# DMA transposes for normalised rows in a two-layer transformer kernel on one Trainium2 core

## The chip, the core and the metric

The kernel runs on one core of a Trainium2 chip. The core has a matrix engine (TensorE, PE in the profile; its weight loads are PEld), a vector engine (VectorE, DVE), an activation engine (ScalarE, ACT), GpSimd (POOL) and a queue engine (SyncE, SP) that issues DMAs here. The engines run side by side, each works off its own instructions in order, and they wait for one another through semaphores. SBUF is the on-chip memory, PSUM the smaller memory into which the matrix engine writes. The metric is the device time of one execution in microseconds (us).

## What is computed

Two layers on x of 2048 rows by 448 columns in bf16; both layers use the same weights. Each layer adds self-attention with 16 heads of 28, and then a two-matrix MLP with a squared relu:

```python
def _layernorm(x, axis=-1, eps=1e-5):
    m = jnp.mean(x, axis=axis, keepdims=True)
    v = jnp.var(x, axis=axis, keepdims=True)
    return (x - m) / jnp.sqrt(v + eps)

# A: softmax(q k^T * Dh**-0.5) v, all heads, times wo
# B: h = x @ w1 + b1;  h = max(h, 0)**2;  h @ w2 + b2
x = x + A(_layernorm(x));  x = x + B(_layernorm(x))
x = x + A(_layernorm(x));  x = x + B(_layernorm(x))
```

## The kernel before

**Tiles.** The 2048 rows are 16 row tiles of 128. Four row tiles make a block of 512 rows; layer 1 cuts its last block in two of two row tiles each. x stays in SBUF (`x_sb`). Heads are padded to 32 rows and lie four to a group, so there are four groups (`g`).

**Attention.** Scores are made transposed: for each group of heads, each block of queries and each key tile, PE multiplies K with Q (L531) into `sc`, a PSUM tile that takes three products of 512 columns. There are two such tiles. ACT takes the exponential of one whole tile, 128x1536, into `pt` (L546); this happens 683 times. PE then multiplies `pt` with V (L581) and sums over keys in one PSUM bank, `oT`. The softmax's denominator comes out of the same product, from a column of ones in V. When a pass ends, DVE takes `oT` out (L605, L607), and norm_stream divides: the denominators go out and come back by three small DMAs on SP's queue (`dn`, L638; `scr`, L650; `rec`, L657) with a reciprocal on DVE between (L644), or, for the last block of a layer, over PE and a wide reciprocal on DVE (L623, L629). L667 multiplies.

**The rest of a block.** chain(l, qb) starts when four groups are divided: the output projection with `wo` for each row tile and the addition to x on DVE (L678), layernorm(), the first MLP matrix with relu (L707 on DVE, L705 on ACT) and square (L714), the second matrix and its addition, and then, in layer 0, another layernorm() and the projections to K, V and Q of layer 1. All these matmuls go through mm_tile() and have the line L405. They share one PSUM bank, `mt` (resource R_m); the score tiles serve them too only before the first and after the last exponential.

**layernorm().** For each row tile DVE takes the moments (L309, L310). One reciprocal square root by Newton steps on DVE serves all row tiles of the block (L319 to L328). L372 writes the normalised row into one of four buffers `xn`. For each pair of row tiles, turn() lets PE transpose eight 128x128 pieces into the PSUM bank as `tp` (L347), and DVE or ACT copies them to `xnT` (L357, L355), which is what the next matmuls read. The four `xn` buffers are held in pairs (resource R_xn).

**What sets the order.** The program's order on each engine is written by a planner inside the kernel. Streams (scores, exponentials, PV, loads, chains and so on) yield operations with an engine, a price in us, dependencies, and resources that they acquire and release. The planner keeps a clock per engine and always emits the operation that could start first, by priority where two could; work on PE has to end near the time at which the next scores are due. So a price changes where an operation stands, not how long it takes. DMAs have the extra latency `LAT["DMA"]` of 2.0 and their own `lat`. All DMAs are issued on SP's queue, one after another, each after its own wait.

**Heat.** The stream heat() adds matmuls without use (L750, they read `xn0` and the identity) where the planned load of PE over the last 2.8 us is under 0.74.

**Loads.** loads() issues x of the first block, wqkv, x of the other blocks, and then wo, w1, b1, w2, b2, all at the start.

Of the kernel before, what the change touches and what calls it, by code (L numbers as in the profile page):

```python
# [10 lines left out]
DT = mybir.dt  # L11
AF = mybir.ActivationFunctionType
ALU = mybir.AluOpType
P = 128
# [9 lines left out]
AHEAD = range(2)  # L24
SLACK = 0.6
WINDOW = 2.8


class Res:
# [9 lines left out]


class Op:
    __slots__ = ("eng", "dur", "fn", "deps", "acq", "rel", "mode", "sets", "start", "end", "res", "turn", "ready", "lat")

    def __init__(self, eng, dur, fn, deps=(), acq=None, rel=None, mode="full", sets=(), lat=0.0):
# [8 lines left out]
LAT = {"PE": 0.22, "ACT": 0.22, "DVE": 0.10, "POOL": 0.15, "DMA": 2.0}  # L53


class Planner:
# [1 line left out]


    def __init__(self):  # L60
        self.clock = {"PE": 0.0, "ACT": 0.0, "DVE": 0.0, "POOL": 0.0, "DMA": 0.0}
        self.mode = None
        self.tok = {}
        self.streams = []
        self.past = []
# [35 lines left out]
    def run(self):  # L101
        while self.streams:
            cands = []
            for st in self.streams:
                s, e = self.earliest(st[2]) if st[2] is not None else (None, None)
                if s is not None:
                    cands.append((s, st[0], e, st))
            assert cands, "no stream can go on"

            due = next((c[3][2].ready for c in cands if c[1] == 0), None)  # L110
            if due is None:
                due = next((c[0] + c[3][2].dur + LAT["ACT"] for c in cands if c[1] == 1), None)
# [12 lines left out]
            if e == "PE":  # L125
                self.mode = o.mode
                self.past = [p for p in self.past if p[1] > s - 8.0] + [(s, o.end)]
            o.fn(e) if o.fn else None
            for a in o.rel:
                a.res.rel[a.turn] = o.end + LAT[e]  # L130
            for key in o.sets:
                self.tok[key] = o
            st[2] = next(st[1], None)
            if st[2] is None:
                self.streams.remove(st)
# [3 lines left out]
def kernel(  # L139
# [12 lines left out]
    nc = tc.nc  # L152
# [95 lines left out]
    def loads():  # L248
        kb = 1024
        yield dma(x_sb[:, 0:2, :], x_view[:, 0:2, :], 224 * kb, ("x", 0, 0))  # L250
        yield dma(x_sb[:, 2:4, :], x_view[:, 2:4, :], 224 * kb, ("x", 0, 1))
        qk_main = A_wqkv[0:3 * P, 0:2 * D].rearrange("(c p) n -> p c n", p=P)
        yield dma(st_qk[:, 0:3, :], qk_main, 680 * kb, ("wqk", 0))
        yield dma(st_qk[0:DL, 3, :], A_wqkv[3 * P:D, 0:2 * D], 112 * kb, ("wqk",))
        v_main = A_wqkv[0:3 * P, 2 * D:3 * D].rearrange("(c p) n -> p c n", p=P)
        yield dma(wv[:, 0:3, :], v_main, 340 * kb, ("wv", 0))
        yield dma(wv[0:DL, 3, :], A_wqkv[3 * P:D, 2 * D:3 * D], 56 * kb, ("wv",))
        for b in range(1, NTB // 4):
            for hf in range(2):
                t0 = 4 * b + 2 * hf  # L260
                yield dma(x_sb[:, t0:t0 + 2, :], x_view[:, t0:t0 + 2, :], 224 * kb, ("x", b, hf))
        for hh in range(G):
            yield dma(wo[DHP * hh:DHP * hh + DH, :, :],
                      A_wo.rearrange("(g hh r) d -> hh r g d", hh=G, r=DH)[hh], 98 * kb, ("wo", hh))
        yield dma(w1[:, 0:3, :], B_w1[0:3 * P, :].rearrange("(c p) n -> p c n", p=P), 1344 * kb, ("w1", 0))
        yield dma(w1[0:DL, 3, :], B_w1[3 * P:D, :], 224 * kb, ("w1", 1))
        yield dma(w1[DL:DL + 1, 3, :], B_b1.rearrange("(o f) -> o f", o=1), 30 * kb, ("w1",))
        yield dma(w2[:, :, :], B_w2.rearrange("(c p) d -> p c d", p=P), 1568 * kb, ("w2",))
        yield dma(b2w[0:1, :], B_b2.rearrange("(o d) -> o d", o=1), 30 * kb, ("b2",))
# [28 lines left out]

    s_left = [True]

    def layernorm(t0, nt, deps_of, early=False):


        mv = sp.tile([P, 4, 2], DT.float32, name="mv")
        last = None
        for j in range(nt):
            def stats(e, j=j):
                st = sp.tile([P, 6], DT.float32, name="st")
                nc.vector.bn_stats(out=st[:, :], in_=x_sb[:, t0 + j, :])  # L309
                nc.vector.bn_aggr(out=mv[:, j, :], in_=st[:, :])  # L310
            last = Op("DVE", 0.80, stats, deps=deps_of(j))
            yield last
        rstd = sp.tile([P, 4], DT.float32, name="rstd")

        def rsqrt(e):
# [46 lines left out]

        for p0 in range(0, nt, 2):
            js = range(p0, min(p0 + 2, nt))
            own = Op("DVE", 0.0, None, acq=R_xn)
            yield own
            xs = []
            for j in js:
                xn = xns[2 * (own.turn % 2) + j % 2]

                def norm(e, j=j, xn=xn):
                    nc.vector.tensor_scalar(out=xn[:, 0:D], in0=x_sb[:, t0 + j, :],  # L372
                                            scalar1=mv[:, j, 0:1], scalar2=rstd[:, j:j + 1],
                                            op0=ALU.subtract, op1=ALU.mult)
                nm = Op("DVE", 0.42, norm, deps=[rs])
                yield nm
                xs.append((xn, nm))

            todo.append((p0, own, xs))
            if early and p0 + 2 < nt:  # L380
                continue
            while todo:
                p0, own, xs = todo.pop(0)
                yield from turn(p0, own, xs)
# [92 lines left out]

    def first_block(blk):
        early = blk == 0
        xnT, own_xt, ends = yield from layernorm(4 * blk, 4, lambda j: [("x", blk, j // 2)] + ([] if early else [GATE[blk]]), early)  # L480
        yield from qkv(0, 4 * blk, 4, xnT, own_xt, ends, early)


# [56 lines left out]
    def e_stream():  # L540
        for gi, us in enumerate(groups):
            n = len(us) * 512

            def fn(e, gi=gi, n=n):
                pt = gbuf[gi]["pt"] = ptp.tile([P, 3 * 512], DT.bfloat16, name="pt")
                nc.scalar.activation(out=pt[:, 0:n], in_=gbuf[gi]["sc"][:, 0:n], func=AF.Exp, scale=scale)  # L546
            o = gbuf[gi]["e"] = Op("ACT", n / 1200 + 0.092, fn, deps=[("s", gi)], acq=R_pt,
                                   rel=gbuf[gi]["s"], sets=("e", gi))
            yield o

# [3 lines left out]
    def p_stream():  # L554
# [11 lines left out]
        for si, ((pi, kb), parts) in enumerate(steps):  # L566
# [8 lines left out]
            def fn(e, kb=kb, parts=parts, box=box, opens=opens, l=l, g=g, kbs=kbs, r=r, n=n):  # L575
                if opens:
                    box["t"] = ps_o.tile([P, QB], DT.float32, name="oT")
                for i in range(r):
# [5 lines left out]
                                         start=(kb + i == kbs[0]), stop=(kb + i == kbs[-1]),  # L584
                                         tile_position=(0, DHP * hh))
            gis = sorted({p[0] for p in parts})
            o = Op("PE", 0.24 + 0.01 * r, fn,
                   deps=[("e", gis[-1]), *{("V", l, kb + i) for i in range(r)}],
                   acq=R_o if opens else None,
                   rel=[gbuf[gi]["e"] for gi in gis if last_use[gi] == si], mode="col")  # L590
# [90 lines left out]
    def chain(l, qb):  # L681
# [13 lines left out]
        yield own_h  # L695
        hacts = []
# [23 lines left out]
        ys = []  # L720
# [75 lines left out]
```

## Time and profile before

| what | value |
|---|---|
| runs | 973.53, 973.73, 972.98 us; median 973.53 |
| the profiled execution | 972.86 us, of which its span on the core 971.1 us |
| granted TensorE clock, mean | 0.993 |
| transposes on PE, L347 | 256 of 128x128, 20.2 us busy |
| scores, L531 | 269.3 us busy on PE |
| PV, L581 | 206.2 us busy on PE |
| matmuls without use, L750 | 291, 93.2 us busy |
| relu on DVE, L707 | 99, 691 ns each |
| moments, L309 and L310 | 64 each, 602 and 182 ns |
| DMA | 16.75 MB, mean 17 GB/s; 273 GB/s in the first fortieth of the span |

The page gives for each group of instructions the busy time and the mean of one, then the idle time of its engine just before it and what ended most of that. Instructions overlap at their ends, so a mean can be longer than the distance from one start to the next. A timeline line gives the start, the time until the last of the merged instructions ended, engine and line, the tiles, the count, and in brackets the idle time before it with its releaser. SPq lines are the issues on SP's queue. In the view by stretch, each pair is busy time and count for PE, PEld, DVE, ACT and POOL, followed by the granted PE clock, the DMA share and GB/s.

### The profile page before, as it was taken

To read this page: it belongs to the slowest core of one execution; us is meant where nothing else is said; L and a number is where in the kernel's file an instruction comes from. 1 tells how busy PE (TensorE), PEld (TensorE's weight loads), DVE (VectorE), ACT (ScalarE), POOL (GpSimd) and SP (SyncE) were. 2 spreads that over 40 slices of the span, in tenths; PEclk is the share of its full clock that TensorE was granted. 3 is DMA by queue.
4 is the path that set the end of the run, shared out by engine and by line. 5 is a ranking of instruction groups with operands and counts; after the bars stand their busy time and mean duration, and the time that the engine had idled before them with its cause. 6 is when DMAs were issued, how large, how long until landed. Compare 5 with 4: busy or idle time off the path is not lost.

```text
span 971.1 us, 16019 instructions
## 1 busy us (share of the span) xinstructions
PE 876.7 (90%) x6701; PEld 303.5 (31%) x6701; DVE 417.9 (43%) x934; ACT 933.5 (96%) x705; POOL 7.6 (1%) x16
## 2 busy tenths in 40 slices
PE   8889989998988999888989899999999998888997
PEld 3233223233222332222322233323233232332345
DVE  7744325525354144553344434426514520344254
ACT  5999999999999999999999999999999999999982
POOL 3000000000000000000000000000000000000000
PEclk9999999999999999999999999999999999999999
DMA  9000010000000000000000000010000000000000
GB/s 273 3 1 1 2 46 1 11 12 13 12 12 3 11 12 13 1 1 1 1 1 1 1 2 1 13 35 24 12 26 17 4 19 21 19 7 13 16 6 20
DMA packets 19732, 16.75 MB, mean 17 GB/s; under 512 B 8394, under 2 KB 16139, under 8 KB 19660
## 3 DMA queue, kind: packets, MB, share of 16 engines
q1 hardware_dynamic: 19660, 15.74, 5.4%
q8 instruction: 52, 0.85, 0.4%
q14 instruction: 20, 0.16, 0.1%
HBM read 13.47 MB, written 2.05 MB: 16 GB/s over the span
## 4 chain that ended last, share of the span: by engine, by line
ACT 58%; issue 19%; PE 17%; DVE 4%; DMA 2%; SPq 0%; ACTq 0%; DVEq 0%
ACT pt L546 57%; PE mt L405 5%; PE sc L531 4%; PE mt L750 3%; PE oT L581 3%; PE sc L405 2%; DVE r L707 1%; DMA part_sb<-in_A_wqkv_dram 1%; DVE rec L629 1%; PE tp L347 1%; DMA rec<-scr 0%; DVE x_sb L678 0%; DMA dn<-oT_sb 0%; DVE st L309 0%; DVE xnT L357 0%
## 5 line engine op out<-in xcount | busy, mean ns | idle before, releaser
L546 ACT ACTIVATE pt<-sc 128x1536 bf16<-128x1536 f32 (+1 forms) x683 | 918.6, 1623 | 7.5 <-PE sc L531 7.3
L531 PE MATMUL sc<-Q_sb,K_sb 32*128 32x512 bf16 (+1 forms) x2304 | 269.3, 360 | 44.6 <-ACT pt L546 34.8
L581 PE MATMUL oT<-pt,V_sb 128*32 128x512 bf16 (+1 forms) x2304 | 206.2, 366 | 0.6 <-ACT pt L546 0.4
L531 PEld LDWEIGHTS <-K_sb 32*128 32x128 bf16 x2304 | 83.8, 91 | 299.8 <-issue 288.2
L405 PE MATMUL mt<-xnT,w 128*128 128x512 bf16 (+1 forms) x424 | 115.2, 376 | 16.5 <-DVE r L707 9.9
L707 DVE TENSOR_SCALAR r<-mt 128x512 bf16<-128x512 f32 x99 | 68.4, 691 | 114.3 <-PE mt L405 114.1
L678 DVE TENSOR_TENSOR x_sb<-x_sb,mt 128x448 bf16<-128x448 bf16 x60 | 37.2, 620 | 152.2 <-PE mt L405 152.2
L750 PE MATMUL mt<-xn,ident 128*128 128x448 bf16 x291 | 93.2, 356 | 8.6 <-DVE r L707 1.8
L405 PE MATMUL mt<-w,h 128*128 128x448 bf16 x406 | 96.1, 358 | 1.6 <-DVE rec L629 0.4
L581 PEld LDWEIGHTS <-V_sb 128*32 128x32 bf16 x2304 | 53.9, 93 | 117.5 <-issue 117.0
L405 PEld LDWEIGHTS <-w 128*128 128x128 bf16 x504 | 42.3, 97 | 63.4 <-issue 46.8
L405 PEld LDWEIGHTS <-h 128*128 128x128 bf16 x448 | 36.5, 98 | 47.0 <-issue 25.6
L714 DVE TENSOR_TENSOR h<-r 128x512 bf16<-128x512 bf16 x112 | 47.4, 423 | 6.8 <-ACT r L705 3.6
L405 PE MATMUL mt<-xnT,wq 128*128 128x512 bf16 x124 | 35.8, 380 | 6.5 <-DVE Q_sb L421 4.5
L309 DVE BATCH_NORM_STATS2 st<-x_sb 128x6 f32<-128x448 bf16 x64 | 38.6, 602 | 0.8 <-DMA x_sb<-in_A_x_dram 0.8
L421 DVE CAST Q_sb<-mt 128x512 bf16<-128x512 f32 x30 | 20.6, 688 | 39.4 <-PE mt L405 39.4
L421 DVE CAST K_sb<-mt 128x512 bf16<-128x512 f32 x30 | 20.7, 691 | 37.2 <-PE mt L405 37.2
L405 PE MATMUL mt<-xnT,wk 128*128 128x512 bf16 x120 | 33.1, 388 | 2.2 <-DVE K_sb L421 0.5
L357 DVE COPY xnT<-tp 128x1024 bf16<-128x1024 bf16 x30 | 20.7, 691 | 31.0 <-PE tp L347 30.9
L667 DVE TENSOR_TENSOR oTn<-oT_sb,rec 128x512 bf16<-128x512 f32 (+1 forms) x36 | 22.4, 622 | 26.7 <-DMA rec<-scr 26.5
L750 PEld LDWEIGHTS <-ident 128*128 128x128 bf16 x291 | 20.1, 97 | 43.0 <-issue 41.9
L405 PE MATMUL mt<-wo,oTn 128*128 128x448 bf16 x124 | 30.3, 353 | 3.3 <-DVE x_sb L678 1.6
(74 smaller groups left out, 347.1 us busy)
## 6 DMA issues: line engine op xcount, KB each, us to landing
rec<-scr SPq DMA_DIRECT2D x24, 256.0 KB
x_sb<-in_A_x_dram SPq DMA_DIRECT2D x8, 224.0 KB
out_dram<-x_sb SPq DMA_DIRECT2D x16, 112.0 KB
w<-in_B_w_dram SPq DMA_DIRECT2D x1, 1568.0 KB
w<-in_B_w_dram SPq DMA_DIRECT2D x1, 1344.0 KB
part_sb<-in_A_wqkv_dram SPq DMA_DIRECT2D x1, 672.0 KB
rec<-scr SPq DMA_DIRECT2D x4, 128.0 KB
wo<-in_A_wo_dram SPq DMA_DIRECT2D x4, 98.0 KB
```

The costliest lines, as they stand in the source:

```text
L309: nc.vector.bn_stats(out=st[:, :], in_=x_sb[:, t0 + j, :])
L357: nc.vector.tensor_copy(out=dst, in_=tp[:, :, 0:w])
L405: nc.tensor.matmul(box["t"][:, c0:c0 + n], lhsT=lhsT, rhs=rhs, start=a, stop=b)
L421: nc.vector.tensor_copy(out=dst, in_=src)
L531: nc.tensor.matmul(sc[:, c0:c0 + nt * P], lhsT=K_sb[l][rows, g, (kb + i) * P:(kb + i + 1) * P], rhs=Q_sb[rows, g, t0 * P:(t0 + nt) * P], s ...
L546: nc.scalar.activation(out=pt[:, 0:n], in_=gbuf[gi]["sc"][:, 0:n], func=AF.Exp, scale=scale)
L581: nc.tensor.matmul(box["t"][DHP * hh:DHP * hh + DHP, 0:n], lhsT=V_sb[l][:, kb + i, 4 * g + hh, :], rhs=gbuf[gi]["pt"][:, c0:c0 + n], start ...
L667: nc.vector.tensor_tensor(out=oTn_of[l, qb][0][:, g, 0:n], in0=res["t"][:, 0:n], in1=box["r"][:, 0:n], op=ALU.mult)
L678: nc.vector.tensor_tensor(out=x_sb[:, tb, :], in0=x_sb[:, tb, :], in1=t[:, 0:D], op=ALU.add)
L707: nc.vector.tensor_scalar(out=r[:, 0:w], in0=t[:, 0:w], scalar1=0.0, scalar2=None, op0=ALU.max)
L714: nc.vector.tensor_tensor(out=h[:, 0:w], in0=r[:, 0:w], in1=r[:, 0:w], op=ALU.mult)
L750: nc.tensor.matmul(t[:, 0:D], lhsT=ident[:, :], rhs=xns[0][:, 0:D], start=True, stop=True)
```

## The change

layernorm() no longer calls turn() unless it is told to (`by_array`): each normalised row tile of 128x448, padded to 512, is turned by one DMA on SP's queue (`dma_start_transpose`) from `xn` straight to its part of `xnT`. The first block of layer 0 and the last block of layer 1 (`LAST`) keep the array. The planner prices such a DMA at 0.3 on the queue and 0.4 + 2.0 until its data is there; the pair of `xn` buffers is free again when both transposes have ended (`need`, `got`).

The moments of a row tile are taken right after its row was added to x, between the projections of the block, instead of all together behind the last one (`moments`, `stats`); the additions and the moments themselves stay as they were. The first-layer blocks still take them in layernorm().

loads() waits with wo and all that follows until K of block 3's first row tile is planned (`("K", 0, 0, 12)`).

The prices of an exponential and of a PV step get smaller, and heat() and the waits of loads() use a clock `"-"` that belongs to no engine.

```diff
+LAST = (1, 4)
...
+        self.need, self.got = need, []
...
             for a in o.rel:
-                a.res.rel[a.turn] = o.end + LAT[e]
+                a.got.append(o.end + o.lat + LAT[e])
+                if len(a.got) == a.need:
+                    a.res.rel[a.turn] = max(a.got)
...
+        yield Op("-", 0.0, None, deps=[("K", 0, 0, 12)])
         for hh in range(G):
             yield dma(wo[DHP * hh:DHP * hh + DH, :, :],
...
-    def layernorm(t0, nt, deps_of, early=False):
...
-        last = None
-        for j in range(nt):
-            def stats(e, j=j):
-                st = sp.tile([P, 6], DT.float32, name="st")
-                nc.vector.bn_stats(out=st[:, :], in_=x_sb[:, t0 + j, :])
-                nc.vector.bn_aggr(out=mv[:, j, :], in_=st[:, :])
-            last = Op("DVE", 0.80, stats, deps=deps_of(j))
-            yield last
+    def moments():
+        return sp.tile([P, 4, 2], DT.float32, name="mv"), []
+
+    def stats(mv, t0, j, deps):
+        def fn(e):
+            st = sp.tile([P, 6], DT.float32, name="st")
+            nc.vector.bn_stats(out=st[:, :], in_=x_sb[:, t0 + j, :])
+            nc.vector.bn_aggr(out=mv[0][:, j, :], in_=st[:, :])
+        o = Op("DVE", 0.80, fn, deps=deps)
+        mv[1].append(o)
+        return o
+
+    def layernorm(t0, nt, deps_of, early=False, by_array=False, mv=None):
+        if mv is None:
+            mv = moments()
+            for j in range(nt):
+                yield stats(mv, t0, j, deps_of(j))
+        last = mv[1][-1]
+        mv = mv[0]
...
-            own = Op("DVE", 0.0, None, acq=R_xn)
+            own = Op("DVE", 0.0, None, acq=R_xn, need=1 if by_array else len(js))
...
+                if by_array:
+                    continue
+
+                def over(e, j=j, xn=xn):
+                    nc.sync.dma_start_transpose(out=xnT[:, :, j * P:(j + 1) * P], in_=xn[:, :])
+                o = Op("DMA", 0.3, over, deps=[nm], rel=own, lat=0.4)
+                yield o
+                ends.append(o)
+            if not by_array:
+                continue
...
-            o = gbuf[gi]["e"] = Op("ACT", n / 1200 + 0.092, fn, deps=[("s", gi)], acq=R_pt,
+            o = gbuf[gi]["e"] = Op("ACT", n / 1200 + 0.068, fn, deps=[("s", gi)], acq=R_pt,
...
-            o = Op("PE", 0.24 + 0.01 * r, fn,
+            o = Op("PE", 0.23 + 0.01 * r, fn,
...
-        adds = []
+        mv = moments()
         for j in range(nt):
             a = yield from mm_tile(
                 [(0, D, [(oTn[:, g, j * P:(j + 1) * P], wo[:, g, :]) for g in range(G)])],
                 add_to_x(t0 + j), 0.62, [*norm_done[l, qb], *[("wo", i) for i in range(G)]])
-            adds.append(a)
+            yield stats(mv, t0, j, [a])
         yield Op("DVE", 0.0, None, deps=[a], rel=own_on)
-        xnT, own_xt, ends = yield from layernorm(t0, nt, lambda j: [adds[j]])
+        xnT, own_xt, ends = yield from layernorm(t0, nt, None, False, (l, qb) == LAST, mv)
...
-            ys.append(a)
+            if l == 0:
+                yield stats(mv, t0, j, [a])
...
         if l == 0:
-            xt2 = yield from layernorm(t0, nt, lambda j: [ys[j]])
+            xt2 = yield from layernorm(t0, nt, None, mv=mv)
             yield from qkv(1, t0, nt, *xt2)
...
-            yield Op("POOL", 0.0, None, deps=[("s", gi)])
+            yield Op("-", 0.0, None, deps=[("s", gi)])
```

More of the change, by code (lines that the diff above doesn't have):

```diff
@@ L41, with __init__ @@
 class Op:
-    __slots__ = ("eng", "dur", "fn", "deps", "acq", "rel", "mode", "sets", "start", "end", "res", "turn", "ready", "lat")
-    def __init__(self, eng, dur, fn, deps=(), acq=None, rel=None, mode="full", sets=(), lat=0.0):
+    __slots__ = ("eng", "dur", "fn", "deps", "acq", "rel", "mode", "sets", "start", "end", "res", "turn", "ready", "lat", "need", "got")
+    def __init__(self, eng, dur, fn, deps=(), acq=None, rel=None, mode="full", sets=(), lat=0.0, need=1):
         self.eng = eng if isinstance(eng, tuple) else (eng,)
@@ L50, in __init__ @@
         self.start = self.end = self.res = self.turn = None
-LAT = {"PE": 0.22, "ACT": 0.22, "DVE": 0.10, "POOL": 0.15, "DMA": 2.0}
+        self.need, self.got = need, []
+LAT = {"PE": 0.22, "ACT": 0.22, "DVE": 0.10, "POOL": 0.15, "DMA": 2.0, "-": 0.0}
 class Planner:
     def __init__(self):
-        self.clock = {"PE": 0.0, "ACT": 0.0, "DVE": 0.0, "POOL": 0.0, "DMA": 0.0}
+        self.clock = {"PE": 0.0, "ACT": 0.0, "DVE": 0.0, "POOL": 0.0, "DMA": 0.0, "-": 0.0}
         self.mode = None
@@ L299 @@
     s_left = [True]
-    def layernorm(t0, nt, deps_of, early=False):
-        mv = sp.tile([P, 4, 2], DT.float32, name="mv")
-        last = None
-        for j in range(nt):
-            def stats(e, j=j):
-                st = sp.tile([P, 6], DT.float32, name="st")
-                nc.vector.bn_stats(out=st[:, :], in_=x_sb[:, t0 + j, :])
-                nc.vector.bn_aggr(out=mv[:, j, :], in_=st[:, :])
-            last = Op("DVE", 0.80, stats, deps=deps_of(j))
-            yield last
+    def moments():
[15 more added lines that the diff above has]
+        mv = mv[0]
         rstd = sp.tile([P, 4], DT.float32, name="rstd")
@@ L479, in first_block @@
         early = blk == 0
-        xnT, own_xt, ends = yield from layernorm(4 * blk, 4, lambda j: [("x", blk, j // 2)] + ([] if early else [GATE[blk]]), early)
+        xnT, own_xt, ends = yield from layernorm(4 * blk, 4, lambda j: [("x", blk, j // 2)] + ([] if early else [GATE[blk]]), early,
+                                               early)
         yield from qkv(0, 4 * blk, 4, xnT, own_xt, ends, early)
@@ L719, in chain @@
         yield Op("DVE", 0.0, None, deps=[o], rel=own_xt)
-        ys = []
+        mv = moments()
         for j in range(nt):
```

## The prediction, made before the changed kernel ran

> **What bounds the kernel now.** I read the page first, for the shares.
>
> ```profile
> span 971.1 us, 16019 instructions
> PE 876.7 (90%) x6701; PEld 303.5 (31%) x6701; DVE 417.9 (43%) x934; ACT 933.5 (96%) x705; POOL 7.6 (1%) x16
> L546 ACT ACTIVATE pt<-sc 128x1536 bf16<-128x1536 f32 (+1 forms) x683 | 918.6, 1623 | 7.5 <-PE sc L531 7.3
> L357 DVE COPY xnT<-tp 128x1024 bf16<-128x1024 bf16 x30 | 20.7, 691 | 31.0 <-PE tp L347 30.9
> ```
>
> ScalarE's 683 exponentials fill 918.6 of 971.1 us. PE looks busy too, but part of that is L750, junk matmuls that keep its clock up. The view that decides is ACT's timeline: when the exponentials start, stop and pause. Two starts from the chain of waits stand below it.
>
> ```profile
> 14.73 6.82 ACT L546 ACTIVATE pt<-sc 128x1536 bf16<-128x1536 f32 x5 [0.49 <-PE sc L531]
> 25.31 13.65 ACT L546 ACTIVATE pt<-sc 128x1536 bf16<-128x1536 f32 x10 [3.75 <-PE sc L531]
> 39.40 365.72 ACT L546 ACTIVATE pt<-sc 128x1536 bf16<-128x1536 f32 x272 [0.45 <-PE sc L531]
> 405.77 28.32 ACT L546 ACTIVATE pt<-sc 128x1536 bf16<-128x1536 f32 x21 [0.65 <-PE sc L531]
> 463.32 477.03 ACT L546 ACTIVATE pt<-sc 128x1536 bf16<-128x1536 f32 x355 [1.30 <-PE sc L531]
> ...
> 81.00 1.17 ACT pt L546
> 82.33 1.16 ACT pt L546
> ```
>
> The span is three pieces: 14.7 us of start; an unbroken run of exponentials to 940.4 (463.32 + 477.03); 30.7 us of tail. In the run one exponential follows the next after 477.03 / 355 = 1.344 us, and after 1.33 where nothing disturbs (82.33 - 81.00). So the run can lose its pauses (3.75 at 21.6, then 0.45, 0.65, 0.33, 0.34 and 1.30, the last five together 3.07) and at most 683 x 0.013 = 9 us of small lags. No normalisation work lies on this path unless it makes PE late with the next scores. The third view, busy time by stretch (PE first, its clock as PEclk), shows what made one pause:
>
> ```profile
> 394.00:398.00 4.00, 3.98 (x29) 1.17 (x27) 2.12 (x5) 4.00 (x4) 0.00 (x0) 1.00 0.02 4
> 398.00:401.46 3.46, 1.79 (x21) 0.69 (x20) 3.43 (x2) 3.46 (x4) 0.00 (x0) 1.00 0.01 2
> 401.46:404.87 3.41, 3.17 (x21) 1.47 (x19) 1.01 (x2) 3.41 (x3) 0.00 (x0) 0.50 0.00 0
> ```
>
> PE busy for only 1.79 of 3.46 us is followed by 3.41 us at clock 0.50, and that by the 0.65 us pause at 405.77. The pauses at 39.4, 434 to 436 and 463.3 lie behind such stretches as well (granted clock 0.51, 0.67 and 0.57 in them). A PE that waits pays twice.
>
> **The change, part by part.** Sums are made on the profiled span; the median of the runs, 973.53, is 2.4 us above it, added at the end.
>
> *Removed.* Of 64 row tiles 6 keep the array path (first block, last block); 58 go over DMA. That takes 232 of 256 transposes from PE (0.62 us per eight, so 18 us) and 29 PSUM copies of 0.69 us (20 us) from DVE. Neither engine ends the run, and PE's order in the changed program refills the gap: 330 junk matmuls instead of 291, 39 x 0.19 = 7.4 us. What is gained is waits on L357: 0.7 us of L405 and 0.3 us of L750 in the table of waits, -1.0 us. Ends: 0, and at most the 3.07 us of pauses on top plus a part of the 9 us.
>
> *Added: a DMA latency under a fixed PE order.* The planner fixes where PE's first consumer of xnT stands; if the data is not there, all of PE queues behind it: the next scores first, then PV, then ACT. So I counted the room the order gives. Example, the MLP of the third block of layer 0: between its last output projection and its first w1 matmul stand seven score groups. The seventh starts 6 x 1.344 = 8.06 us after the first; with its own 0.32 us and two junk matmuls (0.38) the consumer is reached 8.8 us after the projection. DVE needs of this 0.1 handover, 0.62 add, 0.77 moments (0.59 + 0.18), 2.3 for the reciprocal root (18.33 to 20.59 in DVE's timeline) and 1.3 for four norms (0.39 + 3 x 0.30): 5.1. Left after the last norm: 3.7 us. The same count gives 3.7 to 4.4 for all twelve normalisations behind the first 70 us; I use 4.0. Three more, blocks 1 to 3 at the start, have over 2.5 us to spare beyond their landing and cost nothing.
>
> No transpose by DMA is in the trace. The nearest rows are the copies on the same SP queue, DVE's wait behind each marking the landing:
>
> ```profile
> 164.81 0.54 SPq L638 DMA_DIRECT2D dn<-oT_sb  x1
> 167.18 0.24 DVE L644 RECIPROCAL dn<-dn 128x16 f32<-128x16 f32 x1
> ...
> 654.51 0.53 SPq L657 DMA_DIRECT2D rec<-scr  x1
> 659.37 0.69 DVE L667 TENSOR_TENSOR oTn<-oT_sb,rec 128x512 bf16<-128x512 f32 x1 [0.56 <-DMA rec<-scr]
> ```
>
> 8 KB from SBUF to SBUF: 2.37 us from issue to use, 0.54 us on the queue. The 256 KB broadcast: 4.86 us, so 2.5 us for its bytes, 1.25 for the 128 KB of one transpose. Four transposes stand in a row, and the first norm ends 0.9 us before the last.
> Low end, priced like the small copy: the fourth issues 0.1 + 3 x 0.54 behind the first norm, 0.8 behind the last, and lands 0.8 + 2.4 = 3.2 us behind it: 0.8 early, free.
> High end, priced like the broadcast: 0.1 + 3 x 1.25 + 2.37 + 1.25 = 7.5 behind the first norm, 6.6 behind the last: 2.6 late.
> By route it is the small copy, by bytes half the broadcast; both rows are equally near, so I take the middle, spacing 0.9 and landing 3.0: 0.1 + 2.7 + 3.0 - 0.9 = 4.9, which is 0.9 us late.
>
> What a late landing costs: two score tiles exist, so the scores behind the blocked consumer must end two exponentials after the step began: 2.69 - 0.32 (scores) - 0.33 (PV) - 0.87 (the four consuming matmuls) - 0.39 (next scores) = 0.8, less 0.2 for handovers: 0.6 us of cover. Middle: 12 x (0.9 - 0.6) = 3.6 us, and for one in four a stretch at half clock at 3.07 / 4 = 0.8: 2.3. Together 5.9. High: 12 x 2.0 + 12 x 0.8 = 33.
>
> [...]
>
> *SP's queue.* 58 more issues, each waiting for its norm. Behind them stand the reciprocal's DMAs (L638, L650, L657): once the broadcast of a head group waits behind four transposes. Its consumer, L667, has two oT_sb buffers and a pass of 21 exponentials as cover; 0. Without the cover it would be PE's L581 that waits, some 2 us.
>
> *Weight loads put off.* wo, w1, w2 and b2 (9 issues) now stand behind block 3's transposes. First use is wo at the first chain, after 140 us in the old trace; 3.5 MB at the 273 GB/s of the page's first slice take 13 us. Hidden: 0, and it gained nothing before either, since x was already ahead of them in the queue.
>
> *Moments between projections.* Three of four pairs (3 x 0.77 = 2.3 us) leave the chain behind the last projection, but in the run that chain is covered. It counts in the tail, where one pair, 0.77 us, goes.
>
> *Moved by the planner: the start.* The new prices of an exponential and of a PV step, and heat() off the POOL clock, issue nothing of their own; they shift the order, in which everything here is counted. After the fifth exponential the old order has V, PV, K, Q, eight transposes, K, scores; the new one V, K, two junk, PV, Q, K, Q, scores: one more projection (0.87) and 0.38 of junk, less 0.44 for eight transposes: +0.8.
>
> *And the tail.* The old one ends so (PE):
>
> ```profile
> 947.89 2.81 PE L405 MATMUL mt<-w,h 128*128 128x448 bf16 x14
> 952.47 0.70 PE L347 MATMUL sc<-ident,xn 128*128 128x128 bf16 x8 [1.58 <-DVE xn L372]
> 953.01 2.81 PE L405 MATMUL sc<-w,h 128*128 128x448 bf16 x14
> 955.85 1.04 PE L405 MATMUL mt<-xnT,w 128*128 128x256 bf16 x8
> ```
>
> The new order puts one such block of 15 matmuls (3.0 us) ahead of the second wo projection and none between transposes and w1. From the first projection's end at 945.9: 3.0 + 0.87 + 0.1 + 0.62 + 0.77 + 2.36 + 0.62 (an add ahead of the norms) + 0.70 + 0.4 + 1.01 (copy) + 0.2 = 956.6 instead of 955.85: +0.8, the 0.77 saved included.
>
> Sum: 971.1 + 0.8 + 0.8 - 1.0 + 5.9 = 977.6; + 2.4 = **980 us**, slower by 0.7%.
>
> **The rivals.**
> *In time, with relief (faster).* The transposes go at the small copy's price, and the freed DVE lets PE get its PSUM bank back sooner, so that the half-clock stretches go: 971.1 + 0.8 - 1.0 - 3.07 - 1.5 (a sixth of the 9 us) + 2.4, the start as before: 969. For it: 20 us less on DVE, and L707 and L629 among the releasers of PE. Against: three of the four half-clock stretches stand beside the 3.36 us reciprocals (L629), which stay. It decides from a landing under 4.0 us behind the last norm.
> *In time, nothing gained.* 971.1 + 0.8 + 0.8 - 1.0 + 2.4 = 974. For it: PE's work is refilled with junk, ACT's count is unchanged.
> *Late as a broadcast.* The high end, 971.1 + 0.6 + 33 + 2.4 = 1007. For it: packets of a transpose are small pieces, 128 columns of 2 bytes, where the broadcast has 2 KB. Against: nothing else fills the queue (16 GB/s over the span).
> *That it doesn't do what it says* is true of the weight loads, in every case.
>
> **How the numbers follow.** A little late: 0.38; in time with relief: 0.31; in time without: 0.17; late as a broadcast: 0.14. Forecast 980, the first. By 0.2% (2 us, what can be told from no change) faster 0.31, same 0.17, slower 0.52. The range runs from 966, the relief case with twice its share of small lags, to 1006, the broadcast case; the forecast's own is 976 to 988.
>
> **What would show it.** Right: PE's L429 (old L405) idle before its first xnT matmul with a DMA into xnT as releaser, some 12 times near 1 us; four transposes at 0.9 us spacing on SP's queue; more stretches at clock 0.5; the first pause on ACT near 4.8 us instead of 3.75; w1 of the last block some 16 us behind the last exponential. Wrong: no such releaser, and a run of exponentials with fewer pauses than before (in time), or waits of over 2 us at each of the twelve (broadcast). A spacing of several us would break the range upwards.

## The result, and the profile after

The changed kernel takes 1011.5 us (median of four runs, 1009.7 to 1017.8) where the kernel before, on the same chip, takes 973.25 us (four runs, 971.5 to 973.7). The ratio is 1.041, 95% interval 1.036 to 1.046: slower by 4%. The forecast was 980 us with a range of 966 to 1006. The direction and the place were right, the size was not, and the range did not hold the time.

The profiled execution took 1012.25 us, its span 1010.3. Three rows of its page (busy us and mean ns of one, then the idle time of the engine before it and what ended most of it):

```profile
span 1010.3 us, 15761 instructions
...
L571 ACT ACTIVATE pt<-sc 128x1536 bf16<-128x1536 f32 (+1 forms) x683 | 921.2, 1625 | 42.4 <-PE sc L556 37.7
...
L429 PE MATMUL mt<-xnT,w 128*128 128x512 bf16 (+1 forms) x440 | 126.0, 392 | 32.3 <-DMA xnT<-xn 17.5
```

The exponentials (L546 before, L571 now) are as many and as long as they were. What grew is the idle time in front of them, from 7.5 to 42.4 us, and the projections (L405 before, L429 now) have a releaser that the old profile did not know: a DMA into `xnT`. The table of waits (total us, times, longest) says how often:

```profile
ACT pt L571 <- PE sc L556: 37.7, 27, 4.9
...
PE mt L429 <- DMA xnT<-xn: 25.7, 12, 3.0
```

Twelve waits of PE behind the DMA, 25.7 / 12 = 2.1 us each: one for each of the twelve normalisations that the prediction counted, and twice the size it gave them. ACT's timeline shows what follows (start, time until the last of the merged instructions ended; in brackets the idle time before):

```profile
15.20 6.82 ACT L571 ACTIVATE pt<-sc 128x1536 bf16<-128x1536 f32 x5 [0.48 <-PE sc L556]
26.93 138.47 ACT L571 ACTIVATE pt<-sc 128x1536 bf16<-128x1536 f32 x103 [4.91 <-PE sc L556]
...
289.95 1.45 ACT L571 ACTIVATE pt<-sc 128x1536 bf16<-128x1536 f32 x1 [1.76 <-PE sc L556]
291.96 1.45 ACT L571 ACTIVATE pt<-sc 128x1536 bf16<-128x1536 f32 x1 [0.56 <-PE sc L556]
294.02 3.02 ACT L571 ACTIVATE pt<-sc 128x1536 bf16<-128x1536 f32 x2 [0.60 <-PE sc L556]
298.50 2.79 ACT L571 ACTIVATE pt<-sc 128x1536 bf16<-128x1536 f32 x2 [1.46 <-PE sc L556]
```

The long unbroken stretches of before are cut up. From the first exponential's start to the last one's end it was 925.6 us (14.73 to 940.35), now it is 963.2 (15.20 to 978.36): 37.5 of the 39.2 us that the span grew. 1.2 of these are the first pause (4.91 instead of 3.75, as forecast); the other 36 lie in the run, 3.0 us for each normalisation.

One of the twelve in full, from the timeline of all engines around 282 us:

```profile
281.67 1.32 DVE L386 TENSOR_SCALAR xn<-x_sb,mv,rstd 128x448 bf16<-128x448 bf16 x4 [0.33 <-PE mt L776]
282.09 5.16 SPq L396 DMA_TRANSPOSE xnT<-xn  x4
...
286.02 0.40 PE L606 MATMUL oT<-pt,V_sb 128*32 128x512 bf16 x4
288.50 1.02 PE L429 MATMUL mt<-xnT,w 128*128 128x512 bf16 x4 [2.07 <-DMA xnT<-xn]
289.45 0.39 PE L556 MATMUL sc<-Q_sb,K_sb 32*128 32x512 bf16 x3
```

The last norm ends at 282.99. Four transposes occupy SP's queue until 287.25, and the first reader of `xnT` starts at 288.50, 1.25 us after the last issue's end and 5.5 us after the last norm. PE had been ready at 286.4. The scores (L556) stand behind the reader, so ACT pauses for 1.76 us until 289.95. The view by stretch has the second price (pairs of busy time and count for PE, PEld, DVE, ACT, POOL; then the granted clock, the DMA share, GB/s):

```profile
286.40:288.50 2.10, 0.03 (x5) 0.03 (x1) 0.69 (x1) 1.79 (x2) 0.00 (x0) 1.00 0.31 68
288.50:289.80 1.30, 1.30 (x7) 0.41 (x8) 0.24 (x1) 0.00 (x0) 0.00 (x0) 0.99 0.06 6
289.80:293.20 3.40, 2.94 (x14) 0.53 (x11) 0.88 (x2) 2.69 (x2) 0.00 (x0) 0.50 0.00 0
293.20:296.60 3.40, 3.40 (x18) 0.82 (x18) 1.15 (x3) 2.67 (x3) 0.00 (x0) 0.50 0.03 2
```

PE does nothing for 2.1 us, and shortly after it runs at half clock for 10.2 us. Scores that took 0.39 us take 0.61, and three further pauses (0.56, 0.60, 1.46) come out of it. Over the whole run of exponentials the trace has 16 windows of 3.41 us at clock 0.50, where before it had 4.

### The profile page after: what moved, and what is told of

Its sections match the earlier page's. It is cut to its first block, busy times and chain, and to the rows that moved or that the text cites. A ratio compares the mean times of both kernels' runs of the same rounds, so it can differ in the third digit from the quotient of the medians.

```text
span 1010.3 us, 15761 instructions
## 1 busy us (share of the span) xinstructions
PE 891.1 (88%) x6508; PEld 293.6 (29%) x6508; DVE 403.8 (40%) x907; ACT 934.9 (93%) x703; POOL 7.5 (1%) x16
## 4 chain that ended last, share of the span: by engine, by line
ACT 45%; PE 27%; issue 16%; DVE 5%; DMA 5%; SPq 2%; ACTq 0%; DVEq 0%
ACT pt L571 44%; PE mt L429 10%; PE sc L556 6%; PE oT L606 4%; PE mt L776 4%; DMA xnT<-xn 3%; SPq L396 2%; PE sc L429 2%; DMA rec<-scr 1%; DVE x_sb L703 1%; PE oT L234 1%; DVE rec L654 1%; DVE r L732 1%; DVE xn L386 1%; DMA scr<-dn 1%
## 5 line engine op out<-in xcount | busy, mean ns | idle before, releaser
L571 ACT ACTIVATE pt<-sc 128x1536 bf16<-128x1536 f32 (+1 forms) x683 | 921.2, 1625 | 42.4 <-PE sc L556 37.7
L556 PE MATMUL sc<-Q_sb,K_sb 32*128 32x512 bf16 (+1 forms) x2304 | 272.5, 365 | 40.8 <-ACT pt L571 32.3
L606 PE MATMUL oT<-pt,V_sb 128*32 128x512 bf16 (+1 forms) x2304 | 208.8, 372 | 0.4 <-ACT pt L571 0.4
L556 PEld LDWEIGHTS <-K_sb 32*128 32x128 bf16 x2304 | 84.6, 91 | 309.8 <-issue 301.9
L429 PE MATMUL mt<-xnT,w 128*128 128x512 bf16 (+1 forms) x440 | 126.0, 392 | 32.3 <-DMA xnT<-xn 17.5
L776 PE MATMUL mt<-xn,ident 128*128 128x448 bf16 x330 | 108.7, 358 | 12.3 <-DVE r L732 2.4
L429 PE MATMUL mt<-w,h 128*128 128x448 bf16 x420 | 98.0, 354 | 1.7 <-DVE x_sb L703 1.0
L703 DVE TENSOR_TENSOR x_sb<-x_sb,mt 128x448 bf16<-128x448 bf16 x61 | 37.8, 620 | 142.5 <-PE mt L429 141.4
L606 PEld LDWEIGHTS <-V_sb 128*32 128x32 bf16 x2304 | 53.8, 93 | 120.5 <-issue 120.5
L429 PEld LDWEIGHTS <-w 128*128 128x128 bf16 x504 | 43.0, 101 | 86.0 <-issue 64.2
L429 PEld LDWEIGHTS <-h 128*128 128x128 bf16 x448 | 36.1, 97 | 46.6 <-issue 24.7
L429 PE MATMUL mt<-xnT,wq 128*128 128x512 bf16 x120 | 35.1, 381 | 6.7 <-DVE Q_sb L445 4.8
L429 PE MATMUL mt<-xnT,wk 128*128 128x512 bf16 x120 | 32.2, 383 | 10.0 <-DMA xnT<-xn 8.2
L776 PEld LDWEIGHTS <-ident 128*128 128x128 bf16 x330 | 23.6, 97 | 53.4 <-issue 52.3
L429 PE MATMUL mt<-wv,xnT 128*128 128x448 bf16 x124 | 33.0, 382 | 3.6 <-DVE K_sb L445 1.8
L630 DVE COPY oT_sb<-oT 128x512 f32<-128x512 f32 (+1 forms) x26 | 15.8, 608 | 44.2 <-PE oT L606 44.1
```

Source lines behind the costliest of these rows:

```text
L429: nc.tensor.matmul(box["t"][:, c0:c0 + n], lhsT=lhsT, rhs=rhs, start=a, stop=b)
L556: nc.tensor.matmul(sc[:, c0:c0 + nt * P], lhsT=K_sb[l][rows, g, (kb + i) * P:(kb + i + 1) * P], rhs=Q_sb[rows, g, t0 * P:(t0 + nt) * P], s ...
L606: nc.tensor.matmul(box["t"][DHP * hh:DHP * hh + DHP, 0:n], lhsT=V_sb[l][:, kb + i, 4 * g + hh, :], rhs=gbuf[gi]["pt"][:, c0:c0 + n], start ...
L703: nc.vector.tensor_tensor(out=x_sb[:, tb, :], in0=x_sb[:, tb, :], in1=t[:, 0:D], op=ALU.add)
L776: nc.tensor.matmul(t[:, 0:D], lhsT=ident[:, :], rhs=xns[0][:, 0:D], start=True, stop=True)
```

## The experiments

Eleven kernels. The edits are to the changed kernel unless another is named; the ratio is to the kernel before, measured on the same chip in between. "Pauses" is ACT's idle time with the scores as releaser (first pause included), "half clock" the number of 3.41 us windows at clock 0.50 before the last exponential ends; both are of the profiled execution. In e4, e5, e6, e9 and e11 that execution is the slowest of its kernel's (1009.3, 1006.0, 989.9, 997.0 and 981.7 us), so there both counts are likely to lie on the high side.

| kernel | us | ratio, 95% interval | pauses, us | half clock |
|---|---|---|---|---|
| before | 973.25 | | 7.3 | 4 |
| changed | 1011.5 | 1.041 (1.036 to 1.046) | 37.7 | 16 |
| e1 array everywhere | 971.2 | 0.999 (0.998 to 1.000) | 7.5 | 3 |
| e2 measured price | 971.7 | 1.000 (0.998 to 1.001) | 6.1 | 1 |
| e3 junk fills the wait | 1001.9 | 1.032 (1.029 to 1.034) | 32.8 | 3 |
| e4 loads at the start | 1006.6 | 1.035 (1.033 to 1.038) | 37.8 | 17 |
| e5 half-way price | 1002.6 | 1.029 (1.025 to 1.033) | 36.0 | 13 |
| e6 plain copies | 988.4 | 1.015 (1.012 to 1.018) | 20.9 | 10 |
| e7 halves, on e2 | 1031.2 | 1.060, a single run | 61.0 | 23 |
| e8 pairs | 984.7 | 1.012 (1.010 to 1.014) | 13.6 | 3 |
| e9 pairs, measured price | 992.4 | 1.019 (1.016 to 1.022) | 26.6 | 13 |
| e10 as e2, loads at the start | 973.7 | 1.001 (1.000 to 1.003) | 6.7 | 3 |
| e11 pairs, roomy price | 976.4 | 1.003 (1.002 to 1.004) | 14.4 | 9 |

**Which part of the change costs the time?** e1 keeps moments, loads and prices, and takes all 64 row tiles over the array again.

```diff
-    def layernorm(t0, nt, deps_of, early=False, by_array=False, mv=None):
+    def layernorm(t0, nt, deps_of, early=False, by_array=True, mv=None):
```

> The changed kernel with all 58 DMA transposes undone (every block by the array); moments between projections, late weight loads and new prices stay. Theory (all the loss comes from the DMA transposes): 968 to 977 us, ACT pauses in the run of exponentials under 10 us. Rival (the order that the other parts make costs a good share): over 985 us.

It took 971.2 us, no different from before. The whole loss is the DMA transposes', and the rest of the change moves nothing that can be measured, either way.

**Is it the DMA, or the place of its reader?** e2 leaves all 58 transposes and tells the planner what they take: 1.3 us on the queue and 1.2 after it.

```diff
-                o = Op("DMA", 0.3, over, deps=[nm], rel=own, lat=0.4)
+                o = Op("DMA", 1.3, over, deps=[nm], rel=own, lat=-0.8)
```

> DMA transposes kept; the planner prices one at 1.3 us on the queue and 1.2 us to its landing, as the trace of the changed kernel has it, so PE's first use of xnT stands some 2 to 3 us later. Theory (a DMA latency under a fixed PE order that stands too early): PE waits on DMA into xnT fall from 35 us to under 3 us and the time to 968 to 980 us. Rival (the transposes disturb in themselves, by the queue, by traffic or by the clock): still over 990 us.

971.7 us. The first line is the view of L396 in the changed kernel, the second the same in e2 (min, median and max ns on the queue):

```profile
L396 SPq DMA_TRANSPOSE xnT<-xn x58: 1188/1217/1990, 22.6 to 968.9; - x58
```

```profile
L396 SPq DMA_TRANSPOSE xnT<-xn x58: 1188/1217/2649, 23.4 to 935.2; - x58
```

The transposes are as slow as they were; only the planner's order differs, in which the first readers stand two to seven exponentials later. ACT's timeline of e2, the first four starts after an idle time (two more follow, after 0.60 and 0.17 us):

```profile
15.94 6.82 ACT L571 ACTIVATE pt<-sc 128x1536 bf16<-128x1536 f32 x5 [0.49 <-PE sc L556]
26.81 123.69 ACT L571 ACTIVATE pt<-sc 128x1536 bf16<-128x1536 f32 x92 [4.04 <-PE sc L556]
150.65 205.99 ACT L571 ACTIVATE pt<-sc 128x1536 bf16<-128x1536 f32 x153 [0.16 <-PE sc L556]
357.44 79.59 ACT L571 ACTIVATE pt<-sc 128x1536 bf16<-128x1536 f32 x59 [0.80 <-PE sc L556]
```

Unbroken runs of 92 and 153 exponentials are back. So 40 us hung on two numbers in the planner. Transposes that land 5.5 us after the last norm are free if the order puts their first reader late enough, and cost 3 us if the reader stands too early, with the next scores behind it.

**How much of it is half clock?** e3 lets PE do ten matmuls without use right before each first reader of `xnT` (after the hundredth exponential), so that PE waits while working.

```diff
+                    for _ in range(fill):
+                        nc.tensor.matmul(box["t"][:, 0:D], lhsT=ident[:, :], rhs=xns[0][:, 0:D], start=True, stop=True)
```

> The changed kernel, with ten matmuls without use put into the PSUM tile ahead of each first use of xnT, for the twelve normalisations behind the hundredth exponential: PE works 1.9 us of the wait off instead of standing still, the data comes no sooner. Theory (about two fifths of the loss is the half clock that follows PE's idle wait): stretches at clock 0.5 in the run fall from 10 to under 6, 992 to 1003 us. Rival (the half clock goes along with the waits but costs nothing of its own): 1008 to 1014 us.

1001.9 us, with 3 windows at half clock instead of 16. 13 windows gone are worth at least 1011.5 - 1001.9 = 9.6 us, 0.7 us each (at least, since the fill can outlast the landing; by the two ratios to the kernel before it is 9.1). That leaves at most 26 of the run's 36 us for direct waiting, 2.2 us at each normalisation.

**Do the loads matter?** e4 takes out the wait that puts wo and the following loads off.

```diff
-        yield Op("-", 0.0, None, deps=[("K", 0, 0, 12)])
```

> The changed kernel with wo, w1, b1, w2, b2 loaded at the start again, ahead of the first transposes. Theory (the late loads hide nothing and cost nothing): 1009 to 1014 us, the pause after the fifth exponential unchanged at 4.9 us. Rival (3.5 MB ahead of block 1's transposes hold them up): 4 us or more above the changed kernel, with a wait on DMA into xnT in the first 60 us.

1006.6 us, under the expected 1009 to 1014, with an interval that just overlaps the changed kernel's. The first pause was 4.05 us and not the expected 4.9. The rival fell: no reader of `xnT` waits for a DMA in the first 60 us. PE's waits behind the DMA came to 21.9 us in this trace instead of 25.7. The edit also shifts the planner's order, and in e10 below, where nothing is late, the same edit changes nothing. That late loads gained anything is not shown.

**How steep is it?** e5 raises the price on the queue only to 0.65, which puts the reader one exponential later at six of the twelve places (not at all at two, two to six at the rest).

```diff
-                o = Op("DMA", 0.3, over, deps=[nm], rel=own, lat=0.4)
+                o = Op("DMA", 0.65, over, deps=[nm], rel=own, lat=0.4)
```

> Changed kernel, planner's price of a transpose on the queue 0.65 instead of 0.3 us, latency left as it is, so that the first reader of xnT stands on average one exponential later. Counted in the built order as in the prediction, the room after the last norm is 5.1 to 5.7 us at ten of the twelve normalisations and 3.8 to 4.2 at the other two (before this edit 3.7 to 4.4 at all). The four transposes land some 5.4 us after the last norm (measured in the changed kernel). Theory (what is late beyond a cover of about 0.6 us costs, and only that starts half-clock stretches): ten places free, two as expensive as now (3 us each): 974 to 984 us, 2 to 4 half-clock stretches more than before the change at most, waits of PE's xnT matmuls on the DMA about twelve times but small, under 8 us in all. Rival (any wait of PE behind the DMA, however short, is followed by half clock): ten times 1.5 and two times 3: 990 to 997 us.

1002.6 us: both missed, and in two ways. First, ten of the twelve places lost 0.8 to 2.9 us each, 1.6 in the mean (ACT's starts, counted against one every 1.344 us). That is near the rival's figure of 1.5, but not for its reason: at seven of the ten no half-clock window follows. There PE idled 1.2 us in the mean behind the DMA and ACT lost the same 1.2, so the count of the room was too wide again (PE was ready 3.2 to 5.1 us after the last norm at the ten places, the data after 4.5 to 6.7) and the cover of 0.6 us that the prediction counted isn't seen. Second, the other two paused 5.0 and 6.5 us, and neither theory had named them. The timeline of e5 at the second:

```profile
350.85 3.84 SPq L396 DMA_TRANSPOSE xnT<-xn  x3
354.78 0.54 SPq L682 DMA_DIRECT2D rec<-scr  x1
355.38 1.19 SPq L396 DMA_TRANSPOSE xnT<-xn  x1
...
362.92 1.03 PE L429 MATMUL mt<-xnT,wk 128*128 128x512 bf16 x2 [6.40 <-DMA xnT<-xn]
...
364.60 1.45 ACT L571 ACTIVATE pt<-sc 128x1536 bf16<-128x1536 f32 x1 [6.48 <-PE sc L556]
```

With the new price the planner put the 256 KB broadcast of the reciprocals between the third and the fourth transpose. The queue was hardly held up (0.54 us), but the fourth transpose, which otherwise lands 1.2 us after its issue has ended, landed 362.92 - 356.57 = 6.35 us after that. The other place (230 us) has the same order and 4.5 us. So at both places a transpose issued 0.6 us behind the broadcast landed late; what it waited for is not shown.

**Is it the transposing, or 128 KB?** e6 issues a plain copy of the same bytes in the same place, in the changed kernel's order, and leaves out the turning.

```diff
-                    nc.sync.dma_start_transpose(out=xnT[:, :, j * P:(j + 1) * P], in_=xn[:, :])
+                    nc.sync.dma_start(out=xnT[:, :, j * P:(j + 1) * P], in_=xn[:, :].rearrange("p (c n) -> p c n", n=P))
```

> Changed kernel with its order and prices, but each of the 58 DMAs copies the 128x512 row tile straight to xnT, without turning it (the transposition is left out). Same bytes, same queue, same dependencies. Theory (the time on the queue and the landing are those of the transposition, not of 128 KB from SBUF to SBUF): the copies stand near 0.5 to 0.6 us on SP's queue each and land 2 to 3 us after their issue, so the fourth lands under 4 us after the last norm: 972 to 980 us. Rival (bytes and route set it, a plain copy is as slow): spacing of 1.2 us or more, PE waits over 20 us: 1003 to 1013 us.

```profile
L396 SPq DMA_DIRECT2D xnT<-xn x58: 593/610/1894, 22.1 to 947.0; - x58
```

That is e6's view of the same line: half the time on the queue, 0.61 against 1.22 us. The four land 3.6 us after the last norm at four undisturbed places (3.56 to 3.75), against 5.5. But 988 us is not 972 to 980. Even plain copies were late at four places, 4.8 to 5.3 us after the last norm (and 4.3 and 4.7 us at two more); at three of them one of the four copies took longer on the queue (up to 1.9 us), at the fourth, 346.8 us, the copies were issued 1 us after a broadcast's issue had ended and landed 3.5 us after the last issue. The theory holds for the queue and only half for the time.

**What are the 1.22 us made of?** e7 takes e2 and issues each row tile as two transposes of 128x256.

```diff
+                    for c in range(0, 4, 2):
+                        nc.sync.dma_start_transpose(out=xnT[:, c:c + 2, j * P:(j + 1) * P], in_=xn[:, c * P:(c + 2) * P])
```

> The kernel with the planner's price set to the measured one (1.3 us on the queue, 971.7 us), and each transpose of 128x512 issued as two of 128x256. Theory (the 1.22 us on the queue are work for each block, small fixed part): each half takes 0.6 to 0.75 us on the queue, four row tiles land within 1 us of where they did, 970 to 977 us. Rival (a fixed cost for each DMA): each half takes 1.1 to 1.2 us, the last lands some 5 us later, past the room of 4 to 7 us counted in this order at most of the twelve places: 1000 to 1040 us.

1031.2 us, in a single run. The theory fell and the rival stood. e8 goes the other way and turns two row tiles with one DMA of 128x1024, with the changed kernel's prices; for this `xnT` is laid out by row tiles.

```diff
+                    nc.sync.dma_start_transpose(out=xnT[:, p0:p0 + m, :, :].rearrange("p t c n -> p (t c) n"),
+                                                in_=xnq[q.turn % 2][:, 0:m, :].rearrange("p t n -> p (t n)"))
```

> Changed kernel with its prices (0.3 on the queue, 2.4 after it), but the row tiles of a pair stand side by side in SBUF and go over one transpose of 128x1024 (29 instead of 58); xnT is laid out by row tiles. Room in the built order 3.7 to 4.7 us after the last norm, as before this edit. Theory (the queue's 1.2 us are a fixed cost of each DMA, as the halves of 1.24 us each showed): two transposes end 2.6 us behind the second norm, 2.0 behind the fourth, and land some 1.2 us later, 3.2 us after the last norm and inside the room: 971 to 978 us, waits of PE on the DMA under 6 us in all. Rival (the cost is fixed only up to 128x512 and doubles with 128x1024): four times 1.25 us as in the changed kernel, 1003 to 1013 us.

The views of the transposes' line in e7 and in e8:

```profile
L397 SPq DMA_TRANSPOSE xnT<-xn x116: 1167/1237/2142, 23.2 to 994.7; - x116
```

```profile
L397 SPq DMA_TRANSPOSE xnT<-xn x29: 1231/1269/2383, 23.1 to 938.6; - x29
```

128x256, 128x512 and 128x1024 hold the queue for 1.24, 1.22 and 1.27 us: a price for each DMA, whatever its size in this range. Pairs therefore win back 27 us of the changed kernel's 38 without any change of price. At six places the data is there 3.6 to 3.8 us after the last norm. 984.7 us is above the expected 971 to 978, because at the other six the first reader starts 4.1 to 5.2 us after it. At four of these a DMA of the reciprocals goes over the queue within 3.5 us before or right behind the pair, at two none does; no run tells whether that is the cause.

**Does a version beat both?** e9 (pairs at 1.3 and 1.2), e10 (e2 with the loads at the start) and e11 (pairs at 1.3 and 3.2, loads at the start) tried. The first price below is that of e9 and e10, the second that of e11; the last line is gone in e10 and e11.

```diff
+                o = Op("DMA", 1.3, over, deps=[nm], rel=own, lat=-0.8)
...
+                o = Op("DMA", 1.3, over, deps=[nm], rel=own, lat=1.2)
...
-        yield Op("-", 0.0, None, deps=[("K", 0, 0, 12)])
```

> As the kernel with one transpose for a pair, and the planner's price as measured for single row tiles (1.3 us on the queue, 1.2 after it). Room in the built order 3.8 to 5.5 us. Theory: all on time, 969 to 974 us, no gain over the kernel before, because the run of exponentials (1.344 us each) sets the time and has nothing left to give but its start pause. Rival (fewer DMAs and the free array make it faster than before): below 968 us.

> The kernel with the measured price of a transpose (1.3 us on the queue, 1.2 after it; 971.7 us), and wo and the later loads issued at the start again. Room in the built order 4.8 to 10.5 us behind the last norm in the run, 3.8 at the last block. The best candidate for less time than before, since it has few pauses in the run. Theory (the run of exponentials sets the time and its pauses are gone in both): 970 to 973 us, no difference from before. Rival (fewer half-clock stretches and an earlier start beat it): 968 us or less.

> One transpose of 128x1024 for a pair, priced 1.3 us on the queue and 3.2 after it, and the loads at the start. Room in the built order 5.5 to 10.5 us, 4.2 at the last block. The pair's landings in the kernel with the changed kernel's prices were 3.6 to 5.2 us behind the last norm. Theory (what comes late at a pair is late because of the room and the broadcast in front of it, not because of the pair): at least 11 us less than the pair priced 0.3 and 2.4 (984.7), that is 970 to 974 us. Rival (pairs disturb something else, such as the matmuls that read xnT by row tiles): 980 us or more.

No. e9, with 992.4 us where 969 to 974 was expected, is slower than e8, though its readers stand where they did or one or two exponentials later. It loses most at four places; at the first, 230 us, a broadcast again stands between two transposes:

```profile
228.01 1.27 SPq L397 DMA_TRANSPOSE xnT<-xn  x1
229.80 0.55 SPq L683 DMA_DIRECT2D rec<-scr  x1
230.42 1.25 SPq L397 DMA_TRANSPOSE xnT<-xn  x1
236.46 1.01 PE L430 MATMUL mt<-xnT,wk 128*128 128x512 bf16 x2 [3.89 <-DMA xnT<-xn]
```

e10, 973.7 us against 973.05 on its chip, is no different from the kernel before. e11 wins 8 us over e8 with more room and the loads at the start (in e10 the loads alone changed nothing), but stays 0.3% above before and outside its expected 970 to 974. In its profiled execution PE waits once for a DMA, 1.6 us at 238 us, where the second pair was again issued 0.6 us behind a broadcast and landed 4.6 us after its issue; most of the other pauses in the run stand beside a half-clock stretch of 17 us at 436 us.

## Why the prediction was wrong

**Right: the place.** PE's first reader of `xnT` idles with a DMA as releaser, twelve times; the next scores and then ACT queue behind it; stretches at half clock follow. The first pause came as counted, 4.91 us (4.8 forecast); the first exponential itself was 0.5 us later, which was not counted.

**Right by luck: the tail.** It took 31.9 us instead of 30.7 (+0.8 forecast, +1.2 measured), but not by the way that was counted. The last block's w1 stands 15.3 us behind the last exponential, not 16, and that is no later than before (15.5). The rest comes after it:

```profile
993.70 1.87 PE L429 MATMUL sc<-xnT,w 128*128 128x256 bf16 x8 [1.10 <-ACT xnT L369]
```

These eight matmuls took 1.04 us before; here they lie in a half-clock window, 992.9 to 996.3 us. In e2 and e10, whose w1 runs at full clock, the tail is 30.5 us.

**Wrong: the term of 5.9 us for late landings.** It was 12 x 0.3 direct and 2.3 for half clock. Measured, it is some 36: about 26 direct and 10 for half clock. Four links of that step were off, all to the same side:

- *The middle price.* Spacing 0.9 and landing 3.0 gave 4.9 us after the last norm; measured 5.5 (median of eleven, 4.9 to 6.3; at the three latest one of the four transposes held the queue for 1.9 to 2.0 us, and no run shows why). The spacing, 5.16 us for four at 282 us, is the high end's 1.25 and a little more. The landing was better than that end had it: 1.2 us after the queue let go, so 2.5 from the issue's start, where the middle had 3.0 and the high end 2.37 + 1.25. Both rows used for the bracket were plain copies and broadcasts, and e6 shows that a plain copy of the same bytes holds the queue half as long (0.61 against 1.22 us). e7 and e8 show that between 128x256 and 128x1024 the bytes do not enter the time on the queue (1.24, 1.22 and 1.27 us). Halving the broadcast's bytes gave 1.25 by chance.
- *The room.* 4.0 us was counted. PE waited 2.1 in the mean for data 5.5 us after the norm, so it was 3.4.
- *The cover.* 0.6 us was set off against the lateness. e3 leaves ACT up to 2.2 us of direct loss for PE's 2.1, and at the seven places of e5 without half clock ACT lost what PE idled, 1.2 us. The cover is about nil.
- *The half clock.* Its price was right (0.8 us forecast for a stretch, 0.7 in e3), its number was not: 3 stretches forecast, 12 windows more measured. Nine of the twelve waits have one to three windows at or right behind them, three (1.2, 1.3 and 2.4 us) have none; the last section shows what goes with it.

The first three are 0.6 us each, and together they turn 0.3 into 2.1 us. With room and landing so close, a count to within 0.6 us on each side could not tell "free" from "2 us late", and the step that gave three errors of this size a joint range of 976 to 988 was too sure. The rival "Late as a broadcast" put 12 x 2.0 and 12 x 0.8 and came nearest, with 1007, though its landing was late by the wrong amount (6.6 instead of 5.5 us) and its room too wide.

**The other terms.** Mid relief, -1.0: not found. e2 (DMA) and e1 (array) agree to 0.5 us within intervals of over 1, so the array's freed 18 us and DVE's 20 gain nothing, as the rival "In time, nothing gained" said of the mechanism. Moments: nothing, as forecast. Weight loads put off: nothing that can be told from no change, as forecast. SP's queue was costed at 0 for a broadcast behind transposes, and that holds here (the PV products, L606, waited 0.4 us in all, none of it for this); the reverse case, a transpose behind a broadcast, was not looked at. Nothing shows that it cost anything in the changed kernel, where the broadcast stands 1 us or more ahead, but in e5 it cost 5.0 and 6.5 us at two places, and it came back in e9 and e11.

## What to carry to other kernels

When work moves from an engine to a DMA under an order fixed in advance, the order's price for it decides more than the DMA does: here the same transposes cost 38 us at a price of 2.7 us and nothing at their measured 2.5 us with 1.3 of it on the queue, because four in a row add up on the queue (5.16 us at 282 us). Measure both parts (time on the queue, time from there to the first reader) before choosing the place of the reader, and compare the end of the last one of the row, not of the first. And if room and landing are within a microsecond of each other, forecast for both sides and widen the range to the late one: here PE paid once for the wait (2.1 us in the mean) and, at nine of the twelve places, again for its clock (0.7 us a window).

## What the runs showed of the hardware

- A transposing DMA from SBUF to SBUF holds SP's queue for 1.24, 1.22 and 1.27 us at 128x256, 128x512 and 128x1024 in bf16, and its data is usable about 1.2 us later with 128x512 (1.1 to 1.4 in the changed kernel). With 128x1024 it is 1.6 to 1.7 us at six places of e8, but 3.2 us at its last block (3.1 in e9), with no other DMA near. A plain copy of 128x512 holds it for 0.61 us and needs 1.8 to 2.0 us more where undisturbed.
- A transpose whose issue starts 0.6 us after that of a 256 KB broadcast is usable 4.5 to 6.4 us after its own issue ends, at all four places where this came up (two in e5, one each in e9 and e11). In the changed kernel four in a row began 1.55 us after a broadcast, at 356.98, and the last of them, 5.4 us behind it, was on time: 1.27 us after its issue.
- Half clock came in whole windows of 3.41 us: before the end, all stretches at clock 0.50 were 3.41 us long in the trace of the kernel before (four) and 3.41, 6.83 or 10.24 us in that of the changed kernel (eleven). The windows lay on a fixed grid: in each of the two traces all of them started a whole number of 3.41 us apart. How busy PE was in one window of the grid went with the clock of the next. Over the two traces, from 30 us to the last exponential, all 11 windows at full clock in which PE was busy for under 55% were followed by half clock, none of 501 over 66%, and 3 of 10 between. At half clock, the least busy window that full clock followed was 93% busy. So the same wait costs more or less by where it falls. In the changed kernel the wait at 286.4 us lies whole in one window, the longer one at 889.4 is shared by two and brought no half clock (the first pair is PE's):

```profile
286.38:289.79 3.41, 1.34 (x11) 0.43 (x8) 0.92 (x2) 1.81 (x2) 0.00 (x0) 1.00 0.22 46
887.12:890.53 3.41, 2.25 (x24) 0.56 (x23) 0.43 (x1) 3.41 (x3) 0.00 (x0) 1.00 0.47 82
890.53:893.94 3.41, 2.08 (x28) 0.63 (x32) 0.67 (x2) 1.55 (x2) 0.00 (x0) 1.00 0.17 38
```
